# Talking-heads attention with a squared-ReLU FFN: first mixing as 64x64 array tiles, scores by way of DRAM, and one run of mixing work per tile pair

## The chip, the cores and the metric

One core of one Trainium2 chip. The metric is device time in microseconds (us) of one execution. Engine names are those of the profile: PE (matmul), PEld (its weight loads), DVE (VectorE), ACT (ScalarE), POOL (GpSimd), SP (SyncE, which here only issues DMAs). PSUM is the memory that the matmuls write; this kernel uses it as 8 banks. An eviction is the instruction on DVE or ACT that reads a result out of its bank; only then can the program give the bank to another matmul. A stream is the time in which a matmul takes in its columns, and an array mode is the size of the tiles into which the PE array is cut.

## The reference, cut to what matters

```python
# q, k, v: (8 batches, 12 heads, 448, 64); w_pre, w_post: (12, 12)
scores = scale * np.matmul(q, k.transpose(0, 1, 3, 2))
scores = np.einsum('bhij,hg->bgij', scores, w_pre)        # first mixing, over heads
attn = np.exp(scores - np.max(scores, axis=-1, keepdims=True))
attn = attn / (np.sum(attn, axis=-1, keepdims=True) + 1e-09)
attn = np.einsum('bhij,hg->bgij', attn, w_post)           # second mixing, over heads
out = np.matmul(attn, v)
# then, with x = out as (3584, 768):   h = max(x @ w_in, 0);   result = (h * h) @ w_out
```

## The kernel before

The queries of a batch are cut into 45 tiles of 10 queries. A tile has 10 queries x 12 heads = 120 rows of 448 keys. A mixing over heads is then a matmul whose contraction runs over the 120 rows, with a block-diagonal weight. There are 180 steps; each takes a pair of tiles through first mixing, and the pair of two steps earlier (LAG = 2) through second mixing. Scores for a later block, the value matmuls and the FFN are placed between.

```python
def score_pair(b, blk, p):                       # scores of two heads for a block of queries
    ...
    pss = [bank("s_ps") for _ in range(2)]       # bank() takes one of the 8 PSUM banks in turn
    for hh in range(2):
        rs = slice(64 * hh, 64 * hh + 64)
        nc.tensor.matmul(pss[hh][:, 0:S], lhsT=qTs[b][rs, p, ...], rhs=kTs[b][rs, p, :], ...)
    for hh, copy in enumerate((nc.scalar.copy, nc.vector.tensor_copy)):
        copy(out=Sb[(b, blk)][:, 2 * p + hh, :], in_=pss[hh][:, 0:S])

def gather(s):                                   # 10 query rows x 12 heads -> 120 partitions, SBUF to SBUF
    ...
    nc.sync.dma_start(out=g[0:n, :], in_=Sb[(b, blk)][x:x + n // H, :, :])

def mix(pair):                                   # first mixing: one 120x128 matmul a tile
    pss = [bank("m_ps") for _ in pair]
    for ps, s in zip(pss, pair):
        nc.tensor.matmul(ps[:, 0:S], lhsT=pre[0:n, :], rhs=Gs.pop(s)[0:n, :], start=True, stop=True)
    for ps, s in zip(pss, pair):
        nc.scalar.activation(out=e[:, :], in_=ps[:, 0:S], func=ACT.Exp, scale=SCALE, accum_out=sm[:, 0:1])
        nc.vector.reciprocal(out=rc[:, :], in_=sm[:, :])
        nc.gpsimd.tensor_scalar(out=d[:, 0:S], in0=e[:, :], scalar1=rc[:, 0:1], scalar2=-1.0 / S,
                                op0=ALU.mult, op1=ALU.add)

def unmix(pair):                                 # second mixing: rows 0-59 and 64-123 as two row tiles
    us = [bank("at_ps") for _ in range(2)]
    for x, s in enumerate(pair):
        for r in range(R):                       # R = 4
            for y in range(2):
                rows = slice(64 * y, 64 * y + HR)          # HR = 60
                nc.tensor.matmul(us[y][:, c:c + HR], lhsT=d[rows, PR * r:PR * r + P], rhs=post[rows, :], ...)
    ...
    nc.vector.tensor_copy(...)                   # two casts a pair, PSUM to bf16

for ds in range(nd + LAG):                       # the order within a step; fill() places FFN work
    ...
    mix(now2)
    fill(share)
    for w, f in now: f()                         # value matmuls, transposes
    unmix(old2)
    scores_for(ds)
    gathers_for(ds)
    fill(share)
```

The softmax here doesn't subtract the row's maximum and nothing guards it: scores larger than these inputs give would overflow.

## Time and profile before

| | before |
|---|---|
| time, median of 3 | 630.3 us (630.21 to 631.06) |
| profiled span, clock | 626.3 us, 0.964 |
| PE, DVE, ACT, POOL busy | 92%, 68%, 63%, 66% |
| first mixing, 360 matmuls | 366 ns each |
| evictions: cast of second mixing, exponential | 670 ns, 557 ns |

From the page of the profile: the span, the row of PE's busy time, the granted clock and DMA's busy share in 40 slices of the span (tenths), and the chain that ended last, by engine.

```profile
span 626.3 us, 19617 instructions
PE 576.3 (92%) x7530; PEld 323.1 (52%) x7530; DVE 423.2 (68%) x1082; ACT 396.7 (63%) x1196; POOL 410.6 (66%) x615
...
PEclk9666998999999999999999999999999999999899
DMA  9999959679547964587556964587543755322002
...
PE 61%; POOL 15%; ACT 7%; DVE 6%; DMA 5%; issue 3%; SPq 2%; ACTq 0%; DVEq 0%; POOLq 0%
```

PE is busy 92% of the span and holds 61% of the chain. In the first five slices DMA is saturated, and in the second to fourth the granted clock is lowered (0.6 of full speed).

The waits of 110 to 560 us: who waited for whom, total us, times, longest.

```profile
POOL d L325 <- DVE rc L323: 124.9, 72, 4.8
DVE rc L323 <- ACT e_sb L321: 70.3, 158, 1.6
...
PEld L346 <- issue: 39.8, 110, 0.7
...
PE s_ps L295 <- ACT e_sb L321: 2.3, 13, 0.2
...
PE m_ps L317 <- ACT hr L236: 1.5, 2, 0.8
```

PE itself (not PEld) appears only with small totals.

Two stretches in the windows view (start:end, length, then busy us of PE, PEld, DVE, ACT, POOL with counts, granted clock, DMA share, GB/s):

```profile
15.00:30.00 15.00, 6.37 (x42) 1.85 (x43) 6.10 (x15) 7.13 (x22) 3.92 (x6) 0.66 1.00 199
...
110.00:560.00 450.00, 437.98 (x5916) 240.97 (x5915) 338.74 (x851) 315.90 (x961) 313.73 (x460) 1.00 0.63 116
```

And one step on PE in the timeline (start, length, group):

```profile
312.06 0.40 PE L346 MATMUL at_ps<-post,d 60*128 60x60 bf16 x16
312.30 0.35 PE L295 MATMUL s_ps<-kT,qT 64*128 64x448 bf16 x2
312.58 0.55 PE L317 MATMUL m_ps<-G,pre 120*128 120x448 bf16 x2
313.06 1.49 PE L258 MATMUL o_ps<-w,h 128*64 128x384 bf16 x16
```

The lengths overlap (the first group lasts 0.40 us, but the next starts after 0.24), so what a group costs is the distance of starts. First mixing costs 0.48 us here: two streams of 448 columns (187 ns each) and one change of mode (about 95 ns).

### The profile page before, as it was taken

How to read it: one execution, taken by the hardware profiler on the slowest of the kernel's cores; microseconds unless marked ns; L12 is line 12 of the kernel's file. 1: busy time of each engine (PE TensorE's matmuls, PEld its weight loads, DVE VectorE, ACT ScalarE, POOL GpSimd, SP SyncE). 2: the span in 40 equal slices, each digit the busy share in tenths (PEclk: the TensorE clock that was granted, in tenths of full speed). 3: DMA queues.
4: the chain of work that ended last, by engine and by line, in shares of the span. 5: the costliest groups of instructions: out<-in, count | busy, mean ns of one | idle time of the engine just before them, and what ended most of it. 6: DMA issues, size and time to landing. Idle time of an engine off the chain costs nothing.

```text
span 626.3 us, 19617 instructions
## 1 busy us (share of the span) xinstructions
PE 576.3 (92%) x7530; PEld 323.1 (52%) x7530; DVE 423.2 (68%) x1082; ACT 396.7 (63%) x1196; POOL 410.6 (66%) x615
## 2 busy tenths in 40 slices
PE   4467898889999999999999999999999999999897
PEld 3124575645545555545545455545555555555554
DVE  3466886888777677866877677867877677654101
ACT  3456576576677657776677657776678657862320
POOL 6385969876488845895388845896387646872450
PEclk9666998999999999999999999999999999999899
DMA  9999959679547964587556964587543755322002
GB/s 141 196 197 189 183 115 159 123 110 166 136 89 117 160 135 100 101 133 113 118 103 112 157 137 98 97 136 117 122 103 74 129 122 101 75 58 76 15 12 78
DMA packets 90882, 73.64 MB, mean 118 GB/s; under 512 B 6308, under 2 KB 87716, under 8 KB 90788
## 3 DMA queue, kind: packets, MB, share of 16 engines
q1 hardware_dynamic: 51842, 49.57, 35.1%
q0 software_dynamic: 38816, 22.81, 28.2%
q8 instruction: 59, 0.97, 0.6%
q14 instruction: 35, 0.29, 0.1%
q10 hardware_dynamic: 130, 0.01, 0.0%
HBM read 45.63 MB, written 11.01 MB: 90 GB/s over the span
## 4 chain that ended last, share of the span: by engine, by line
PE 61%; POOL 15%; ACT 7%; DVE 6%; DMA 5%; issue 3%; SPq 2%; ACTq 0%; DVEq 0%; POOLq 0%
PE o_ps L258 22%; PE h_ps L228 16%; PE m_ps L317 8%; POOL d L325 6%; PE at_ps L346 5%; POOL h L237 5%; PE ot_ps L181 4%; PE s_ps L295 4%; ACT e_sb L321 3%; ACT xt L192 3%; DMA G<-S 3%; DVE at L353 2%; PE tr_ps L162 2%; DVE S L298 2%; SPq L310 2%
## 5 line engine op out<-in xcount | busy, mean ns | idle before, releaser
L325 POOL TENSOR_SCALAR d<-e_sb,rc 128x448 bf16<-128x448 f32 x360 | 226.6, 641 | 162.3 <-DVE rc L323 159.9
L321 ACT ACTIVATE e_sb<-m_ps 128x448 f32<-128x448 f32 x360 | 195.6, 557 | 77.4 <-PE m_ps L317 64.0
L353 DVE CAST at<-at_ps 112x480 bf16<-112x480 f32 x352 | 221.7, 670 | 32.7 <-PE at_ps L346 31.7
L228 PE MATMUL h_ps<-xt,w 128*128 128x448 bf16 (+2 forms) x960 | 168.5, 317 | 2.8 <-ACT e_sb L321 1.6
L258 PE MATMUL o_ps<-w,h 128*128 128x384 bf16 (+1 forms) x1024 | 162.5, 327 | 1.4 <-POOL h L237 1.3
L237 POOL TENSOR_TENSOR h<-hr 128x448 bf16<-128x448 f32 (+2 forms) x160 | 123.9, 781 | 28.5 <-ACT hr L236 25.8
L228 PEld LDWEIGHTS <-w 128*128 128x128 bf16 x960 | 82.8, 98 | 77.7 <-issue 20.9
L258 PEld LDWEIGHTS <-h 128*128 128x128 bf16 (+1 forms) x1024 | 85.3, 100 | 70.2 <-issue 15.6
L298 ACT CAST S<-s_ps 128x448 bf16<-128x448 f32 x192 | 100.0, 550 | 28.2 <-PE s_ps L295 19.9
L323 DVE RECIPROCAL rc<-sm 128x1 f32<-128x1 f32 x360 | 54.9, 159 | 91.8 <-ACT e_sb L321 89.5
L298 DVE CAST S<-s_ps 128x448 bf16<-128x448 f32 x192 | 112.8, 609 | 5.2 <-PE s_ps L295 2.9
L317 PE MATMUL m_ps<-G,pre 120*128 120x448 bf16 x360 | 104.6, 366 | 12.6 <-DMA G<-S 8.7
L236 ACT ACTIVATE hr<-h_ps 128x448 f32<-128x448 f32 (+2 forms) x136 | 68.5, 504 | 46.8 <-PE h_ps L228 31.0
L346 PEld LDWEIGHTS <-d 60*128 60x128 bf16 x2880 | 53.7, 94 | 62.6 <-issue 46.0
L295 PE MATMUL s_ps<-kT,qT 64*128 64x448 bf16 x384 | 73.6, 370 | 12.4 <-ACT S L298 7.5
L346 PE MATMUL at_ps<-post,d 60*128 60x60 bf16 x2880 | 75.0, 190 | 4.3 <-ACT xt L192 0.9
L321 ACT ACTIVATION_READ_ACCUMULATOR e_sb<-m_ps 128x1 f32 x360 | 78.1, 217 | 0.0
L192 ACT ACTIVATE xt<-ot_ps,bvec 128x160 bf16<-128x160 f32 (+3 forms) x144 | 42.6, 392 | 44.8 <-PE ot_ps L181 31.3
L317 PEld LDWEIGHTS <-pre 120*128 120x128 bf16 x360 | 29.2, 98 | 52.0 <-issue 21.3
L265 DVE COPY osb<-o_ps 128x384 f32<-128x384 f32 x48 | 26.6, 554 | 39.9 <-PE o_ps L258 39.0
L181 PE MATMUL ot_ps<-at,v 112*64 112x160 bf16 (+4 forms) x1152 | 45.9, 240 | 3.5 <-DVE at L353 3.5
L181 PEld LDWEIGHTS <-v 112*64 112x64 bf16 x1152 | 42.2, 117 | 7.6 <-issue 6.8
(36 smaller groups left out, 194.1 us busy)
## 6 DMA issues: line engine op xcount, KB each, us to landing
G<-S SPq DMA_DIRECT2D x352, 105.0 KB
kst<-in_k_dram POOLq DMA_DIRECT2D x24, 224.0 KB, 5.8
qst<-in_q_dram POOLq DMA_DIRECT2D x24, 224.0 KB, 5.9
v<-in_v_dram POOLq DMA_DIRECT2D x24, 224.0 KB, 6.2
w<-in_moe_w_in_dram POOLq DMA_DIRECT2D x8, 384.0 KB, 11.1
w<-in_moe_w_out_dram POOLq DMA_DIRECT2D x8, 384.0 KB, 7.5
out_dram<-osb SPq DMA_DIRECT2D x8, 336.0 KB
out_dram<-osb SPq DMA_DIRECT2D x8, 288.0 KB
```

Source lines behind the costliest of these rows:

```text
L181: nc.tensor.matmul(ps[64 * hh:64 * hh + 64, TW * y + c0:TW * y + 2 + n], lhsT=vs[b][0:PR, g, r, :], rhs=at[0:PR, r, g, c0:2 + n], start=(y ...
L228: nc.tensor.matmul(ps[:, 0:n], lhsT=w1[ft // 4][:, c2, ft % 4 * 128:ft % 4 * 128 + 128], rhs=xts[b][:, c2, c0:c1], start=(c2 == 0), stop=( ...
L236: nc.scalar.activation(out=hr[:, 0:n], in_=ps[:, 0:n], func=ACT.Relu)
L237: nc.gpsimd.tensor_tensor(out=h2ts[(b, ft)][:, c0:c1], in0=hr[:, 0:n], in1=hr[:, 0:n], op=ALU.mult)
L258: nc.tensor.matmul(dst, lhsT=h2ts[(b, ft)][:, mt * 128:mt * 128 + ROWS[mt]], rhs=w2[ft // 4][:, ft % 4, n2 * 384:(n2 + 1) * 384], start=(f ...
L295: nc.tensor.matmul(pss[hh][:, 0:S], lhsT=qTs[b][rs, p, BLK_START[blk]:BLK_START[blk] + P], rhs=kTs[b][rs, p, :], start=True, stop=True)
L298: copy(out=Sb[(b, blk)][:, 2 * p + hh, :], in_=pss[hh][:, 0:S])
L317: nc.tensor.matmul(ps[:, 0:S], lhsT=pre[0:n, :], rhs=Gs.pop(s)[0:n, :], start=True, stop=True)
L321: nc.scalar.activation(out=e[:, :], in_=ps[:, 0:S], func=ACT.Exp, scale=SCALE, accum_out=sm[:, 0:1])
L325: nc.gpsimd.tensor_scalar(out=d[:, 0:S], in0=e[:, :], scalar1=rc[:, 0:1], scalar2=-1.0 / S, op0=ALU.mult, op1=ALU.add)
L346: nc.tensor.matmul(us[y][:, c:c + HR], lhsT=d[rows, PR * r:PR * r + P], rhs=post[rows, :], start=True, stop=True)
L353: nc.vector.tensor_copy(out=dst[:, :, :, y, :], in_=src)
```

## The change

First mixing multiplies by a block-diagonal weight: 5 of a tile's 10 queries never meet the other 5. So half a tile (60 rows) fits one 64-row half of the array, and four such blocks (two tiles, two halves) fit the array at once. The rows must then lie at partitions 0-59 and 64-123. The gather of before was taken to be unable to give that in one access pattern, so scores are stored to DRAM and gathered from there. Second mixing is cut into 64x64 tiles as well, so that first mixing, scores and second mixing share one array mode; they are emitted as one run, and all FFN work of the step follows it.

```diff
 def score_pair(n):
+        for z, m in ((0, 64), (64, QB - 64)):
+            nc.tensor.matmul(pss[hh][z:z + m, 0:S], lhsT=qTs[b][rs, p, q0:q0 + m], rhs=kTs[b][rs, p, :], ...)
     ...
+    if p % 2:
+        nc.sync.dma_start(out=Sd[b][QB * blk:QB * blk + QB, 2 * p - 2:2 * p + 2, :], in_=Sb[0][0:QB, :, :])
 def gather(k):
+    for y in range(2):      # both tiles of the pair, one half of their queries
+        src = Sd[b][IQ * t:IQ * t + 2 * IQ, :, :].rearrange("(x y i) h j -> y (i h) x j", x=2, y=2)
+        nc.sync.dma_start(out=g[64 * y:64 * y + HR, :, :], in_=src[y])
 def mix(k):
-    for ps, s in zip(pss, pair):
-        nc.tensor.matmul(ps[:, 0:S], lhsT=pre[0:n, :], rhs=Gs.pop(s)[0:n, :], ...)
+    for y in range(2):
+        for x in range(2):
+            nc.tensor.matmul(pss[y][64 * x:64 * x + 64, 0:S], lhsT=pre[rows, :], rhs=g[rows, x, :], ...)
 def unmix(k):
-                nc.tensor.matmul(us[y][:, c:c + HR], lhsT=d[rows, PR * r:PR * r + P], rhs=post[rows, :], ...)
+                    for z in (0, 64):
+                        nc.tensor.matmul(us[x][z:z + 64, c:c + HR], lhsT=d[rows, PR * r + z:PR * r + z + 64],
+                                         rhs=post[rows, :], ...)
     ...                                          # within a step:
-            if now2:
-                mix(now2)
-            fill(share)
             for w, f in now:
                 f()
+            if now2:
+                mix(ds)
+            scores_for(ds)
             if old2:
-                unmix(old2)
+                unmix(ds - LAG)
-            scores_for(ds)
             gathers_for(ds)
             fill(share)                          # share is now the whole step's, not half
```

(Cut: constants, the building of the weights, the rule for when scores are due.)

More of the change, by code (lines that the diff above doesn't have):

```diff
@@ L23 @@
 NT = 45
-RG = H * IQ
-TPB = 12
-BLK_START = [0, 120, 240, 320]
-BLK_OFF = [0, 0, 0, 40]
-BLK_TILES = [12, 12, 12, 9]
+QB = 112
 HQ = IQ // 2
@@ L34 @@
 LAG = 2
-AHEAD = 10
+AHEAD = 6
 SCALE = 1.0 / 8.0
@@ L64 @@
     ffnp = ctx.enter_context(tc.tile_pool(name="ffnp", bufs=1))
+    dram = ctx.enter_context(tc.tile_pool(name="dram", bufs=3, space=bass.MemoryType.DRAM))
     psp = ctx.enter_context(tc.tile_pool(name="psp", bufs=8, space=bass.MemoryType.PSUM))
@@ L92, in wcol @@
         return t
-    col_pre = wcol(w_pre, "col_pre", nc.sync, [(0, IQ)])
+    col_pre = wcol(w_pre, "col_pre", nc.sync, [(0, HQ), (64, HQ)])
     col_post = wcol(w_post, "col_post", nc.scalar, [(0, HQ), (64, HQ)])
-    istripe = consts.tile([P, IQ], F32, name="istripe")
-    nc.vector.tensor_reduce(out=istripe[0:RG, :], in_=ident[0:RG, 0:RG].rearrange("p (i h) -> p i h", h=H),
-                            axis=mybir.AxisListType.X, op=ALU.add)
     hstripe = consts.tile([P, HQ], F32, name="hstripe")
@@ L104 @@
                                 axis=mybir.AxisListType.X, op=ALU.add)
-    pre = consts.tile([P, P], BF16, name="pre")
+    pre = consts.tile([P, 64], BF16, name="pre")
     nc.vector.memset(pre[:, :], 0.0)
-    for y in range(2):
-        nc.vector.tensor_tensor(
-            out=pre[0:RG, 64 * y:64 * y + HR].rearrange("p (i g) -> p i g", g=H),
-            in0=istripe[0:RG, HQ * y:HQ * y + HQ].unsqueeze(2).to_broadcast([RG, HQ, H]),
-            in1=col_pre[0:RG, :].unsqueeze(1).to_broadcast([RG, HQ, H]), op=ALU.mult)
     post = consts.tile([P, H, HQ], BF16, name="post")
@@ L115 @@
         ps = slice(p0, p0 + HR)
+        nc.vector.tensor_tensor(out=pre[ps, 0:HR].rearrange("p (i g) -> p i g", g=H),
+                                in0=hstripe[ps, :].unsqueeze(2).to_broadcast([HR, HQ, H]),
+                                in1=col_pre[ps, :].unsqueeze(1).to_broadcast([HR, HQ, H]), op=ALU.mult)
         nc.vector.tensor_tensor(out=post[ps, :, :], in0=hstripe[ps, :].unsqueeze(1).to_broadcast([HR, H, HQ]),
@@ L163, in turn_unit @@
                                         ident[0:PR, 0:PR])
+        if which == 0:
+            turned[b] = 2 * u + 2
         (eng or nc.vector.tensor_copy)(out=store[b][:, 2 * u:2 * u + 2, :],
                                        in_=ps[:, 0:2 * S].rearrange("p (y s) -> p y s", y=2))
+    turned = {}
     def turn_units(b):
@@ L284, in ffn2_units, with score_pair @@
         return u
-    Sb, Gs, dsb = {}, {}, {}
-    def score_pair(b, blk, p):
-        if (b, blk) not in Sb:
-            Sb[(b, blk)] = work.tile([P, H, S], BF16, name="S", tag="S", bufs=2)
+    Sd, Sb, Gs, dsb = {}, {}, {}, {}
+    def score_pair(n):
+        b, blk, p = n // (4 * NPAIR), n // NPAIR % 4, n % NPAIR
+        if b not in Sd:
+            Sd[b] = dram.tile([S, H, S], BF16, name="Sd", tag="Sd")
+        if p % 2 == 0:
+            Sb[0] = work.tile([P, 4, S], BF16, name="S", tag="S", bufs=3)
         pss = [bank("s_ps") for _ in range(2)]
@@ L294, in score_pair @@
             rs = slice(64 * hh, 64 * hh + 64)
-            nc.tensor.matmul(pss[hh][:, 0:S], lhsT=qTs[b][rs, p, BLK_START[blk]:BLK_START[blk] + P],
-                             rhs=kTs[b][rs, p, :], start=True, stop=True)
+            for z, m in ((0, 64), (64, QB - 64)):
+                q0 = QB * blk + z
+                nc.tensor.matmul(pss[hh][z:z + m, 0:S], lhsT=qTs[b][rs, p, q0:q0 + m], rhs=kTs[b][rs, p, :],
+                                 start=True, stop=True)
         for hh, copy in enumerate((nc.scalar.copy, nc.vector.tensor_copy)):
-            copy(out=Sb[(b, blk)][:, 2 * p + hh, :], in_=pss[hh][:, 0:S])
@@ L300, in rows_of @@
-    def rows_of(t):
-        return H * min(IQ, S - IQ * t)
-    def gather(s):
-        b, t = s
-        blk, tl = divmod(t, TPB)
-        n = rows_of(t)
-        x = BLK_OFF[blk] + IQ * tl
-        g = work.tile([P, S], BF16, name="G", tag="G", bufs=AHEAD + 2)
-        nc.sync.dma_start(out=g[0:n, :], in_=Sb[(b, blk)][x:x + n // H, :, :])
-        Gs[s] = g
-    def mix(pair):
-        pss = [bank("m_ps") for _ in pair]
-        for ps, s in zip(pss, pair):
-            n = rows_of(s[1])
-            nc.tensor.matmul(ps[:, 0:S], lhsT=pre[0:n, :], rhs=Gs.pop(s)[0:n, :], start=True, stop=True)
-        for ps, s in zip(pss, pair):
+            copy(out=Sb[0][0:QB, 2 * (p % 2) + hh, :], in_=pss[hh][0:QB, 0:S])
@@ new lines, in score_pair, with queries, needs, gather @@
+        if p % 2:
+            nc.sync.dma_start(out=Sd[b][QB * blk:QB * blk + QB, 2 * p - 2:2 * p + 2, :], in_=Sb[0][0:QB, :, :])
+    def queries(t, y):
+        return max(0, min(HQ, S - IQ * t - HQ * y))
+    def needs(s):
+        b, t = s
+        return 4 * NPAIR * b + NPAIR * ((min(IQ * t + IQ, S) - 1) // QB + 1)
+    def gather(k):
+        (b, t), (b2, t2) = pair = steps[2 * k:2 * k + 2]
+        g = work.tile([P, 2, S], BF16, name="G", tag="G", bufs=AHEAD + 1)
+        for y in range(2):
+            if b == b2 and t2 < NT - 1:
+                src = Sd[b][IQ * t:IQ * t + 2 * IQ, :, :].rearrange("(x y i) h j -> y (i h) x j", x=2, y=2)
+                nc.sync.dma_start(out=g[64 * y:64 * y + HR, :, :], in_=src[y])
+            else:
+                for x, (bx, tx) in enumerate(pair):
+                    q0, n = IQ * tx + HQ * y, queries(tx, y)
+                    nc.sync.dma_start(out=g[64 * y:64 * y + H * n, x, :],
+                                      in_=Sd[bx][q0:q0 + n, :, :].rearrange("i h j -> (i h) j"))
+        Gs[k] = g
@@ L319, in mix @@
+    def mix(k):
+        pss = [bank("m_ps") for _ in range(2)]
+        g = Gs.pop(k)
+        for y in range(2):
+            for x in range(2):
+                rows = slice(64 * y, 64 * y + H * queries(steps[2 * k + x][1], y))
+                nc.tensor.matmul(pss[y][64 * x:64 * x + 64, 0:S], lhsT=pre[rows, :], rhs=g[rows, x, :],
+                                 start=True, stop=True)
+        for y in range(2):
             e = work.tile([P, S], F32, name="e_sb", tag="E", bufs=3)
             sm = work.tile([P, 1], F32, name="sm", tag="sm", bufs=4)
-            nc.scalar.activation(out=e[:, :], in_=ps[:, 0:S], func=ACT.Exp, scale=SCALE, accum_out=sm[:, 0:1])
+            nc.scalar.activation(out=e[:, :], in_=pss[y][:, 0:S], func=ACT.Exp, scale=SCALE, accum_out=sm[:, 0:1])
@@ L322, in mix @@
             rc = work.tile([P, 1], F32, name="rc", tag="rc", bufs=4)
             nc.vector.reciprocal(out=rc[:, :], in_=sm[:, :])
-            d = dts[(NT * s[0] + s[1]) % ND]
+            d = dts[(2 * k + y) % ND]
             nc.gpsimd.tensor_scalar(out=d[:, 0:S], in0=e[:, :], scalar1=rc[:, 0:1], scalar2=-1.0 / S,
                                     op0=ALU.mult, op1=ALU.add)
-            dsb[s] = d
+            dsb[(k, y)] = d
     def place_of(s):
@@ L334, in place_of, with unmix @@
         return ats[(b, part)], 2 + IQ * (t - PARTS[b % 2][part])
-    def unmix(pair):
-        places = [place_of(s) for s in pair]
+    def unmix(k):
+        places = [place_of(s) for s in steps[2 * k:2 * k + 2]]
         us = [bank("at_ps") for _ in range(2)]
-        for x, s in enumerate(pair):
-            d = dsb.pop(s)
+        for y in range(2):
+            d = dsb.pop((k, y))
             for r in range(R):
-                for y in range(2):
-                    rows = slice(64 * y, 64 * y + HR)
-                    c = 4 * HR * x + HR * r
-                    nc.tensor.matmul(us[y][:, c:c + HR], lhsT=d[rows, PR * r:PR * r + P], rhs=post[rows, :],
-                                     start=True, stop=True)
-        (at, c), (at2, c2) = places
-        for y in range(2):
-            src = us[y][0:PR, 0:8 * HR].rearrange("p (x m i) -> p m x i", x=2, i=HQ)
-            if at is at2:
-                dst = at[0:PR, :, :, c:c + 2 * IQ].rearrange("p r g (x z i) -> p (r g) x z i", z=2, i=HQ)
-                nc.vector.tensor_copy(out=dst[:, :, :, y, :], in_=src)
-            else:
-                for x, (a, p) in enumerate(places):
-                    dst = a[0:PR, :, :, p + HQ * y:p + HQ * y + HQ].rearrange("p r g i -> p (r g) i")
-                    nc.vector.tensor_copy(out=dst, in_=src[:, :, x, :])
+                c = HR * (R * y + r)
+                for x in range(2):
+                    rows = slice(64 * x, 64 * x + HR)
+                    for z in (0, 64):
+                        nc.tensor.matmul(us[x][z:z + 64, c:c + HR], lhsT=d[rows, PR * r + z:PR * r + z + 64],
+                                         rhs=post[rows, :], start=True, stop=True)
+        for x, (at, c) in enumerate(places):
+            src = us[x][0:PR, 0:8 * HR].rearrange("p (y m i) -> p m y i", y=2, i=HQ)
+            dst = at[0:PR, :, :, c:c + IQ].rearrange("p r g (y i) -> p (r g) y i", y=2)
+            nc.vector.tensor_copy(out=dst, in_=src)
     filler = []
@@ L374, in fill @@
             owed[0] = min(owed[0], 0.0)
-    blocks = [(b, blk) for b in range(B) for blk in range(4)]
     steps = [(b, t) for b in range(B) for t in range(NT)]
@@ L383 @@
             if x > 0:
-                score_pair(0, 0, 2 * x - 2)
-                score_pair(0, 0, 2 * x - 1)
+                score_pair(2 * x - 2)
+                score_pair(2 * x - 1)
         nc.gpsimd.dma_start(out=wpost_bf[:, :], in_=w_post[0:H, 0:H])
@@ L408 @@
         nd = len(steps) // 2
-        starts = [NT * b + TPB * blk for b, blk in blocks] + [len(steps)]
         issued, gathered = [NPAIR], [0]
+        due = [(0, 0)] + [(min(k for k in range(nd) if max(needs(x) for x in steps[2 * k:2 * k + 2]) > NPAIR * n), NPAIR * n)
+                          for n in range(1, 4 * B)] + [(nd, 4 * B * NPAIR)]
         def scores_for(ds):
-            tile = 2 * ds + AHEAD + 2
-            blk = sum(tile >= x for x in starts) - 1
-            if blk + 1 >= len(blocks):
-                return
-            if blk == 3:
-                want = NPAIR * 4 + 2 * max(0, ds - FIRST_TURN[1])
-            else:
-                into, size = tile - starts[blk] - 2, starts[blk + 1] - starts[blk] - 2
-                want = NPAIR * (blk + 1) + -(-NPAIR * into // size)
-            while issued[0] < min(want, NPAIR * (blk + 2)):
-                score_pair(*blocks[issued[0] // NPAIR], issued[0] % NPAIR)
+            k = ds + AHEAD + 1
+            n = sum(k >= x for x, _ in due)
+            if n >= len(due):
+                want = due[-1][1]
+            elif n in (4, 5):
+                want = due[4][1] + 2 * max(0, ds - FIRST_TURN[1])
+            else:
+                (k0, n0), (k1, n1) = due[n - 1:n + 1]
+                want = n0 + NPAIR + -(-NPAIR * (k - k0) // (k1 - k0)) if n1 < due[-1][1] else n1
+            if n < 4:
+                want = min(want, due[4][1])
+            while issued[0] < min(want, due[-1][1]) and issued[0] % NPAIR < turned.get(issued[0] // (4 * NPAIR), 0):
+                score_pair(issued[0])
                 issued[0] += 1
         def gathers_for(ds):
-            while gathered[0] < min(2 * ds + AHEAD + 2, len(steps)):
-                b, t = steps[gathered[0]]
-                if issued[0] < NPAIR * (4 * b + t // TPB + 1):
+            while gathered[0] < min(ds + AHEAD, nd):
+                if issued[0] < max(needs(x) for x in steps[2 * gathered[0]:2 * gathered[0] + 2]):
                     break
-                gather(steps[gathered[0]])
+                gather(gathered[0])
                 gathered[0] += 1
@@ L452 @@
                 rest = 1 + min(x for x in EARLY if x >= ds) - ds
-            share = sum(w for w, _ in filler) / rest / 2 if now2 else 1e9
+            share = sum(w for w, _ in filler) / rest if now2 else 1e9
             now = timed.pop(ds, [])
-            if now2:
-                mix(now2)
-            fill(share)
             for w, f in now:
```

## The prediction

> What bounds the kernel now. The windows view of 110 to 560 us shows PE 92 to 99% busy, DVE, ACT and POOL 65 to 84%; there the list of waits has almost no PE wait above 10 us except "issue" before weight loads (40 us before second mixing, 15 and 14 before the FFN, 11 before first mixing). In the records of single matmuls this is a change of array mode: the first matmul of the other mode starts about 95 ns after the last one has streamed, some 400 times, about 39 us. The Trainium skill ("TensorEngine Tiling (Array Packing)", Key Properties) says a mode change drains the array; the trace agrees. So the middle is bound by PE streaming plus drains. The first 80 us are not: DMA share 1.0, granted clock down to 0.5, and first mixing waits for gathers.
>
> What the change does.
> 1. First mixing: two matmuls of a pair start 187 to 193 ns apart (128x128, one after the other). As four 64x64 tiles on separate rows and columns they should stream together: minus 187 ns a pair, 180 pairs, 33 us. The trace shows such overlap for two row tiles (scores, 3 ns apart) and two column tiles (transposes, 2 to 3 ns).
> 2. Scores: two matmuls become four, still one stream of 448: no change.
> 3. Second mixing: 16 weight loads and matmuls become 32. Now eight groups at 27.5 ns. The same page says column tiling loses fast weight load; the trace shows 15 ns between loads of one 128-column tile and 28 ns for a 64-column tile, two of them side by side. Eight groups at 28 ns: plus 0 to 10 ns a pair, if the sequencer keeps up with 64 instructions in 225 ns (row-tiled ones come 1.6 ns apart).
> 4. Mode changes: still two a step.
> 5. DVE, ACT, POOL: same numbers and sizes of evictions (670, 609, 550, 557, 641 ns). DVE's chain gets later, since second mixing follows at once: 3.8 us after first mixing against a step of 2.9; PSUM banks are reused about a step later, so this is close.
> 6. DMA: 38.5 MB of stores in 3584-byte packets, estimated at 175 ns from the 154 ns of 3072-byte ones: 10752 of them, 19% of 16 engines. Gathers keep size and number of packets but spread over 15 engines instead of 10, by my reading of the shapes.
> 7. SyncE queue: 360 gathers and 64 output stores at 0.87 and 0.80 us now; then about 370 gathers, 96 score stores and 64 outputs at about 0.96 with its wait: 510 us of 600. Close, but gathers run 15 us ahead.
> 8. Start: the first gather waits for a store's landing, plus 4 to 6 us, and the crowded first 80 us get 5 MB more: plus 2 to 5 us.
>
> Sum: minus 33, plus 2 for second mixing, plus 8 at the start, plus 4 from 5 and 7: about 611 us, range 596 to 630. Chances: faster 0.58, within 2% 0.27, slower 0.15.
>
> Right if: four first-mixing matmuls start within 10 ns and the next kind follows 190 ns later; second mixing spans 0.4 us; middle DMA share 0.8; few waits for gathers after 60 us.
> Wrong if: the sequencer or slow weight loads stretch second mixing to 0.6 us (plus 40 us); SyncE or DMA become the limit, shown as first mixing waiting for gathers throughout; PSUM reuse makes scores or second mixing wait for DVE; or the tiles do not run together.

## More of the kernel before

Groups of instructions on the page: busy us and mean ns of one, then idle time ahead of them and its main releaser.

```profile
L353 DVE CAST at<-at_ps 112x480 bf16<-112x480 f32 x352 | 221.7, 670 | 32.7 <-PE at_ps L346 31.7
...
L317 PE MATMUL m_ps<-G,pre 120*128 120x448 bf16 x360 | 104.6, 366 | 12.6 <-DMA G<-S 8.7
...
L346 PE MATMUL at_ps<-post,d 60*128 60x60 bf16 x2880 | 75.0, 190 | 4.3 <-ACT xt L192 0.9
```

## The result, and the profile after

| | before | after |
|---|---|---|
| median of 4 runs | 630.25 us (629.63 to 631.06) | 655.76 us (652.81 to 657.51) |
| profiled span, clock | 626.3 us, 0.964 | 651.0 us, 0.949 |

The ratio is 1.0399, 95% interval 1.0352 to 1.0446: slower by 4%, where 3% faster was predicted. A ratio here is always the mean time of one kernel's fast runs over that of the other's of the same rounds, so it is not quite the ratio of the medians quoted.

The page of the profile after:

```profile
span 651.0 us, 26878 instructions
PE 572.0 (88%) x11154; PEld 352.6 (54%) x11154; DVE 415.1 (64%) x1073; ACT 394.3 (61%) x1196; POOL 410.3 (63%) x615
...
PEclk9555898789999999999999999999999999999999
DMA  9999978959965995669755995669755576431102
...
PE 45%; POOL 16%; DVE 13%; ACT 10%; DMA 10%; issue 5%; SPq 1%; ACTq 0%; POOLq 0%; DVEq 0%
```

PE is busy about as long as before in a span that is 25 us longer. Its part of the chain fell from 61% to 45%; DVE's rose from 6% to 13%, ACT's from 7% to 10%, DMA's from 5% to 10%. Busy time of DVE, ACT and POOL did not grow: the evictions do not cost more, they are waited for more.

The same groups:

```profile
L367 DVE CAST at<-at_ps 112x480 bf16<-112x480 f32 x360 | 219.0, 642 | 3.6 <-PE at_ps L362 3.6
...
L362 PE MATMUL at_ps<-post,d 60*64 60x60 bf16 x5760 | 95.4, 196 | 14.3 <-ACT S L299 1.8
...
L331 PE MATMUL m_ps<-G,pre 60*64 60x448 bf16 x720 | 83.5, 386 | 21.6 <-DMA G<-Sd 18.3
```

DVE's cast of second mixing was preceded by 32.7 us of idle time waiting for PE; now by 3.6. Before, DVE stood ready when second mixing ended. Now the casts are late, and PE is ahead of them.

The waits of 110 to 560 us after:

```profile
POOL d L340 <- DVE rc L338: 135.1, 78, 5.5
...
DVE rc L338 <- ACT e_sb L336: 61.0, 111, 2.0
DVE S L299 <- PE s_ps L296: 40.9, 39, 2.5
...
PEld L362 <- issue: 24.6, 73, 1.4
...
PEld L331 <- DMA G<-Sd: 8.3, 24, 0.4
...
PE ot_ps L177 <- DVE at L367: 4.9, 5, 1.5
```

Waits for gathers are 8.3 us in 24 pieces of at most 0.4 us, so DMA is not the limit of the middle. The value matmuls now wait for DVE's cast, which is new. PE's other waits are split into many small lines, so the list hides their sum. I add it up below from the starts of single matmuls.

The windows of before, after:

```profile
15.00:30.00 15.00, 1.41 (x14) 0.57 (x18) 0.96 (x3) 1.50 (x5) 0.41 (x1) 0.62 1.13 256
...
110.00:560.00 450.00, 421.44 (x8626) 258.67 (x8628) 323.23 (x823) 302.37 (x932) 301.93 (x447) 0.98 0.77 187
```

From 15 to 30 us PE did 1.41 us of work instead of 6.37: the start waits longer. In the middle PE is less busy, and so is every engine but DMA. The granted clock of 0.98 comes from 110 to 170 us alone (0.82 and 0.94 in its two halves); from 170 to 560 us it is 1.00 in both kernels, so what is said of that stretch below is not the clock.

Two neighbouring steps on PE, behind value matmuls:

```profile
377.62 0.38 PE L331 MATMUL m_ps<-G,pre 60*64 60x448 bf16 x4
377.83 0.36 PE L296 MATMUL s_ps<-kT,qT 64*64 64x448 bf16 x4
378.02 0.45 PE L362 MATMUL at_ps<-post,d 60*64 60x60 bf16 x32
378.35 0.80 PE L331 MATMUL m_ps<-G,pre 60*64 60x448 bf16 x4
379.29 0.38 PE L296 MATMUL s_ps<-kT,qT 64*64 64x448 bf16 x4
379.81 0.21 PE L362 MATMUL at_ps<-post,d 60*64 60x60 bf16 x2
380.24 0.44 PE L362 MATMUL at_ps<-post,d 60*64 60x60 bf16 x30 [0.21 <-ACT S L299]
380.61 2.77 PE L254 MATMUL o_ps<-w,h 128*128 128x384 bf16 x16
```

The first step is what the change was made for: first mixing 0.21 us, scores 0.19, second mixing 0.33, all within 0.73 us. In the records its four mixing matmuls start within 10 ns (so do those of 141 of the 180 steps). No FFN work stands between these two steps, so the pair shows the loss at its worst and not in a usual step. The second step needs six PSUM banks again at once, and takes 2.26 us (380.61 less 378.35) for the same matmuls. DVE and ACT in that time:

```profile
378.27 0.62 DVE L299 CAST S<-s_ps 112x448 bf16<-112x448 f32 x1 [1.99 <-PE s_ps L296]
379.27 0.17 DVE L338 RECIPROCAL rc<-sm 128x1 f32<-128x1 f32 x1 [0.38 <-ACT e_sb L336]
379.35 0.64 DVE L367 CAST at<-at_ps 112x480 bf16<-112x480 f32 x1
379.91 0.15 DVE L338 RECIPROCAL rc<-sm 128x1 f32<-128x1 f32 x1
379.98 0.64 DVE L367 CAST at<-at_ps 112x480 bf16<-112x480 f32 x1
```

```profile
376.90 1.81 ACT L188 ACTIVATE xt<-ot_ps,bvec 128x160 bf16<-128x160 f32 x6 [2.02 <-PE ot_ps L177]
378.58 0.57 ACT L336 ACTIVATE e_sb<-m_ps 128x448 f32<-128x448 f32 x1
...
379.09 0.58 ACT L336 ACTIVATE e_sb<-m_ps 128x448 f32<-128x448 f32 x1
...
379.61 0.58 ACT L299 CAST S<-s_ps 112x448 bf16<-112x448 f32 x1
```

Read together: ACT is still at the value matmuls' results until 378.71, and in the records the second half of first mixing starts at 378.77. ACT's first exponential ends at 379.15; the scores start at 379.29. Its second ends at 379.67; second mixing gets its first bank at 379.81. Its score copy ends at 380.19, and second mixing goes on at 380.24. PE moves one bank at a time, at ACT's pace. On DVE the casts of the step before, whose data was complete by 378.47, stand behind a reciprocal that waits for the exponential: DVE is idle for 0.38 us with two finished banks in its queue, and frees them at 379.99 and 380.62.

**Where the 25 us are.** I took the start of the first exponential of each step from both traces. After runs behind before by 4.8 us at step 0, 12.4 at step 8, 16.0 at step 48, 28.1 at step 168, and 24.7 at the end. So there are two losses: 16 us up to step 48, and 12 us over the 120 steps after that, where the change should have gained 21.

For these 120 steps I split PE's time from the records of single matmuls: "stream" is columns / 2.4 in ns (448 columns take 187 to 188 ns in the trace before), divided by the number of tiles that work side by side; "mode changes" is 95 ns each; "rest" is what remains of the distance between starts.

| steps 48 to 168, us | total | stream | mode changes | rest | of it waits over 60 ns |
|---|---|---|---|---|---|
| before | 370.6 | 316.4 | 25.4 | 28.9 | 14.8 |
| after | 382.7 | 295.1 | 21.1 | 66.4 | 42.5 |

The stream fell by 21 us and the mode changes by 4; the rest grew by 37.5. Of first mixing's stream 44.8 us became 22.4, which is 187 ns a step. For each wait over 60 ns I looked up which instruction of DVE, ACT or POOL had just ended. Before: exponentials 4.9 us, value evictions 3.3, score copies 2.8, casts of second mixing 0.8. After: casts of second mixing 15.2, exponentials 11.9, ACT's score copies 6.1, value evictions 5.5. Of the 15.2, 5.6 us stand ahead of the value matmuls, which read what the cast wrote; that is a wait for data and not for a bank. The attribution is by coincidence in time, so I tested it.

Where in the emission the waits fall is as telling. After, 84 of the 120 steps stand alone between two stretches of FFN work; their runs hold only 7.5 us of the 42.5 (about 90 ns a step). The other steps follow one another without FFN work between, almost all in 15 stretches of two or three steps together with the value matmuls; these hold 26 us. The rest, 8 us, is in the FFN work. Before, the 16 stretches with value matmuls hold 9 us.

### The profile page after: what moved, and what is told of

Its sections match the earlier page's. It is cut to its first block, busy times and chain, and to the rows that moved or that the text cites. A ratio compares the mean times of both kernels' runs of the same rounds, so it can differ in the third digit from the quotient of the medians.

```text
span 651.0 us, 26878 instructions
## 1 busy us (share of the span) xinstructions
PE 572.0 (88%) x11154; PEld 352.6 (54%) x11154; DVE 415.1 (64%) x1073; ACT 394.3 (61%) x1196; POOL 410.3 (63%) x615
## 4 chain that ended last, share of the span: by engine, by line
PE 45%; POOL 16%; DVE 13%; ACT 10%; DMA 10%; issue 5%; SPq 1%; ACTq 0%; POOLq 0%; DVEq 0%
PE o_ps L254 19%; PE h_ps L224 11%; DVE at L367 7%; POOL d L340 6%; ACT e_sb L336 6%; POOL h L233 6%; DMA Sd<-S 5%; DMA G<-Sd 4%; PE ot_ps L177 4%; PE m_ps L331 4%; PE at_ps L362 3%; ACT xt L188 3%; DVE S L299 2%; PE s_ps L296 2%; PE tr_ps L154 2%
## 5 line engine op out<-in xcount | busy, mean ns | idle before, releaser
L224 PE MATMUL h_ps<-xt,w 128*128 128x448 bf16 (+2 forms) x960 | 165.2, 325 | 4.3 <-ACT S L299 1.8
L254 PE MATMUL o_ps<-w,h 128*128 128x384 bf16 (+1 forms) x1024 | 158.1, 327 | 2.8 <-POOL h L233 1.9
L299 DVE CAST S<-s_ps 112x448 bf16<-112x448 f32 x192 | 116.6, 615 | 53.2 <-PE s_ps L296 45.2
L224 PEld LDWEIGHTS <-w 128*128 128x128 bf16 x960 | 85.7, 102 | 57.4 <-issue 2.1
L362 PEld LDWEIGHTS <-d 60*64 60x64 bf16 x5760 | 87.1, 112 | 52.8 <-issue 35.3
L362 PE MATMUL at_ps<-post,d 60*64 60x60 bf16 x5760 | 95.4, 196 | 14.3 <-ACT S L299 1.8
L299 ACT CAST S<-s_ps 112x448 bf16<-112x448 f32 x192 | 101.7, 549 | 7.9 <-DMA Sd<-S 7.9
L331 PE MATMUL m_ps<-G,pre 60*64 60x448 bf16 x720 | 83.5, 386 | 21.6 <-DMA G<-Sd 18.3
L296 PE MATMUL s_ps<-kT,qT 64*48 64x448 bf16 (+1 forms) x768 | 80.4, 381 | 12.3 <-ACT S L299 4.2
L331 PEld LDWEIGHTS <-pre 60*64 60x64 bf16 x720 | 26.8, 105 | 70.8 <-issue 34.0
```

Source lines behind the costliest of these rows:

```text
L224: nc.tensor.matmul(ps[:, 0:n], lhsT=w1[ft // 4][:, c2, ft % 4 * 128:ft % 4 * 128 + 128], rhs=xts[b][:, c2, c0:c1], start=(c2 == 0), stop=( ...
L254: nc.tensor.matmul(dst, lhsT=h2ts[(b, ft)][:, mt * 128:mt * 128 + ROWS[mt]], rhs=w2[ft // 4][:, ft % 4, n2 * 384:(n2 + 1) * 384], start=(f ...
L296: nc.tensor.matmul(pss[hh][z:z + m, 0:S], lhsT=qTs[b][rs, p, q0:q0 + m], rhs=kTs[b][rs, p, :], start=True, stop=True)
L299: copy(out=Sb[0][0:QB, 2 * (p % 2) + hh, :], in_=pss[hh][0:QB, 0:S])
L331: nc.tensor.matmul(pss[y][64 * x:64 * x + 64, 0:S], lhsT=pre[rows, :], rhs=g[rows, x, :], start=True, stop=True)
L362: nc.tensor.matmul(us[x][z:z + 64, c:c + HR], lhsT=d[rows, PR * r + z:PR * r + z + 64], rhs=post[rows, :], start=True, stop=True)
```

## The experiments

The theories, with the letters that the texts use: A, the order is at fault: one run asks for six banks within 0.8 us, and evictions cannot keep pace. (From e3 on the texts part two forms of it: the bare number of banks in one run, and the queue form, in which evictions stand in DVE's order behind reciprocals that wait for the exponentials.) B, the way through DRAM. C, the 64x64 tiles themselves, by slow weight loads or too many instructions. D, too few buffers behind the exponentials. All kernels were timed against the kernel before on the same chip (629.0 to 629.4 us, median of 7), and all gave results within the comparison's tolerance, also those that leave arithmetic out. By the record's rule (2%), after, e4, e5, e7 and e9 are slower than before, e1 and e13 unclear, and all others the same; smaller differences below rest on the 95% intervals given. "Middle" is the length of steps 48 to 168 in the profiled run: 370.6 us before, 382.7 after.

### e1: the change with the order of before

```diff
-            share = sum(w for w, _ in filler) / rest if now2 else 1e9
+            share = sum(w for w, _ in filler) / rest / 2 if now2 else 1e9
+            if now2:
+                mix(ds)
+            fill(share)
             for w, f in now: ...
-            if now2:
-                mix(ds)
-            scores_for(ds)
             if old2: ...
+            scores_for(ds)
```

> The changed kernel with the emission order of before (first mixing, fill, second mixing, scores, fill) and the fill share halved again. Theory A (the one run asks for six PSUM banks within 0.8 us, so PE waits for evictions): the waits at second mixing fall from 29 us to about 8 in steps 48 to 168, two more mode changes a step (190 ns, 23 us in these steps) come back; about 635 to 645 us in all. Theory B (the way through DRAM costs the time, at the start and by load): no gain, 652 us or more. Theory C (the 64x64 tiles are slow by themselves): no gain either, second mixing stays at 0.5 us a group.

640.79 us, ratio 1.0182 (1.0149 to 1.0216); middle 373.1, with waits over 60 ns down from 42.5 to 23.3 us and about one more mode change a step (32.0 us instead of 21.1). As A expected (635 to 645 us): the one-run order costs 2.2% (1.0399 less 1.0182), some 14 us, more than the mode changes that it saves. But 1.8% remain.

### e2: only the scores' way through DRAM

The kernel before, its matmuls and its order, with scores stored to DRAM and each tile's 120 rows gathered from there (blocks of 112 queries and the rule for when scores are due are those of after):

```diff
+        if p % 2:
+            nc.sync.dma_start(out=Sd[b][QB * blk:QB * blk + QB, 2 * p - 2:2 * p + 2, :], in_=Sb[0][...])
-        nc.sync.dma_start(out=g[0:n, :], in_=Sb[(b, blk)][x:x + n // H, :, :])
+            nc.sync.dma_start(out=g[0:n, :], in_=Sd[b][IQ * t:IQ * t + n // H, :, :].rearrange("i h j -> (i h) j"))
```

> Scores through DRAM alone: matmuls, modes and order of before, gathers of 120 rows from DRAM. Theory A: the first 40 steps lose 12 to 17 us as in the changed kernel, the rest runs as before; 643 to 648 us. Theory B: also slower in steps 48 to 168, 650 us or more. If the way through DRAM costs nothing: 630 us.

637.19 us, ratio 1.0139 (1.0110 to 1.0169), less than expected. It lags by 6.1 us at step 0, 11.4 at step 6 and still 10.4 at step 168; its middle is 370.2, as before. So the way through DRAM costs 9 us, all at the start, and nothing later. From e2 to e1 it is then another 0.4%, under 3 us, and the intervals overlap: the tiles in the old order bring no gain and no clear loss. From e1 to after 2.2%. These three parts make up the 4.0%.

### e3: the run turned round

Second mixing, then scores, then first mixing, so that first mixing's banks are emptied while the FFN streams:

```diff
-            if now2:
-                mix(ds)
-            scores_for(ds)
             if old2:
                 unmix(ds - LAG) ...
+            scores_for(ds)
+            if now2:
+                mix(ds)
```

> The changed kernel with the run turned round: second mixing, scores, first mixing. The evictions of second mixing and scores then do not queue behind the reciprocals that wait for the exponentials. Theory A in the form that the VectorE queue behind the reciprocals holds the banks: PE waits for PSUM fall by half or more, 625 to 640 us. If only the number of banks in one run matters: within 1% of 655. Theories B and C: 655.

637.73 us, ratio 1.0141 (1.0124 to 1.0158); middle 371.6, rest 55.7. The same instructions, tiles and mode changes as after, in another order inside the run, are 16 us faster. That is the strongest evidence that the order costs the time, and it is within what the queue form of A expected. The other form falls: this run, too, asks for six banks at once, and for it 655 us were expected. Of the 16 us, 11 are in the middle. The text also expected the waits for PSUM to fall by half; all waits over 60 ns fall only from 42.5 to 34.9 us. Its waits of 110 to 560 us show what came instead:

```profile
DVE at L367 <- PE at_ps L362: 60.6, 70, 2.5
...
PEld L362 <- POOL d L340: 20.6, 47, 0.9
```

DVE waits for second mixing again, as in before. But second mixing now waits for POOL's scaling of the exponentials, which has less time, since second mixing stands first in the run and first mixing last. Of the waits over 60 ns (34.9 us), 8.8 end with that scaling, 6.1 with exponentials, 5.3 with value evictions, 5.2 with casts and 5.0 with POOL's squares.

### e4: second mixing as the row tiles of before

```diff
-                    for z in (0, 64):
-                        nc.tensor.matmul(us[x][z:z + 64, c:c + HR], lhsT=d[rows, PR * r + z:PR * r + z + 64], ...)
+                    nc.tensor.matmul(us[x][:, c:c + HR], lhsT=d[rows, PR * r:PR * r + P], ...)
```

> The changed kernel with second mixing as 16 row tiles of 64x128 as before; one more mode change a step. Theory C (small tiles cost): second mixing falls from 250 to 220 ns of pure stream and from 0.5 us to 0.3 a group in all, so faster than 655 by 10 us or more. Theory A: one more mode change of 95 ns a step, partly hidden in waits: 655 to 668 us.

652.47 us, ratio 1.0372 (1.0352 to 1.0392), not clearly apart from after and outside what either theory expected (A 655 to 668). Second mixing's rest falls from 29.0 to 15.1 us, but one more mode change a step takes 13 us of it back (34.3 instead of 21.1), and the middle is 383.9. C falls as the main cause. The tiles do have a price: where nothing waits, the median group of second mixing takes 43 ns more than its stream would (74 ns of rest, as in the median group of e3, instead of 31, the median before), and first mixing's 17 ns (26 instead of 9). Over 120 steps that is 7 us.

### e5 and e6: the first FFN weight loaded later, in after and in before

```diff
-            at_load(-1 if x < 4 else x - 4, load_w1, x)
+            at_load(2 * x + 1, load_w1, x)
```

> The changed kernel with the eight loads of the first FFN weight spread over tiles 1 to 15 instead of being issued before and in the first four tiles. If the loss at the start is DMA load (stores and gathers queue with the weight loads): the first exponential comes at 25 us or earlier instead of 28.7, the lead of the kernel before at step 8 falls from 12 us to 6 or less, 648 us or less in all. If it is the bare round trip through DRAM: no change at step 0, 655 us.

> Control: the same shift of the weight loads in the kernel before. If its own first gathers (6.3 us from issue to first use) also queue behind the loads: 2 to 4 us faster, about 626 us. If not, 629 us. A loss would mean that the weights come too late for the first FFN units.

e5: 650.96 us, ratio 1.0354 (1.0306 to 1.0402). e6: 634.79, ratio 1.0088 (1.0071 to 1.0106). The first exponential starts at 22.4 us in e5 and at 21.6 in e6, against 28.7 and 23.8 with the early loads. With these loads out of the way the whole change costs 0.8 us at step 0 and 0.6 at step 8, instead of 4.8 and 12.4. So the loss at step 0 is for the most part not the bare round trip but its queueing behind the weight loads, while DMA is at its limit. (At step 8 both kernels wait: e5 lags 6.7 us behind before and e6 6.1, so the 0.6 shows less.) In all, both missed: 648 us or less was expected of e5, and about 626 of e6, or 629. The loss cannot simply be moved: e6 lags 7.4 us behind before at step 48. That the weights came too late, as the text feared, its trace does not show: the first FFN matmul starts at 61.9 us (before 61.0) and waits for no weight. What e6 waits for is gathers: on the chain of work that ended last one takes 8.3 us from 41.4 us (in before 3.6 from 40.1), while the loads land, and one 6.6 us from 81.4 us, after they have landed, when the lag grows from 0.9 to 5 us. Why this second one is late stays open. (Between e5 and e6 4.4 us have come up by step 48, against 16.0; the rest is in the middle as before, 383.0 against 370.4.)

### e7 and e8: lighter evictions

No accumulator read on ACT, the reciprocal taken of a constant, casts of half the columns; in after (e7) and in before (e8).

```diff
-            nc.scalar.activation(out=e[:, :], in_=..., func=ACT.Exp, scale=SCALE, accum_out=sm[:, 0:1])
+            nc.scalar.activation(out=e[:, :], in_=..., func=ACT.Exp, scale=SCALE)
-            nc.vector.reciprocal(out=rc[:, :], in_=sm[:, :])
+            nc.vector.reciprocal(out=rc[:, :], in_=one[:, :])
-            nc.vector.tensor_copy(out=dst, in_=src)
+            nc.vector.tensor_copy(out=dst[:, 0:2 * H], in_=src[:, 0:2 * H])
```

> Wrong result on purpose: the changed kernel with lighter evictions. The reciprocal takes a constant instead of the sum of the exponentials (no accumulator read on ScalarE, no wait on it in VectorE's queue) and the casts after second mixing copy half the columns. PE work is untouched. Theory A (evictions hold the PSUM banks, PE waits): PE waits over 100 ns in steps 48 to 168 fall from 51 us to under 15, 615 to 628 us in all. Theory C (64x64 matmuls are slow by themselves): 650 us or more.

> Wrong result on purpose: the same lighter evictions in the kernel before. Theory A: its PE waits are only 18 us in these steps, so it gains 5 to 15 us, 615 to 625 us, and the changed kernel with the same evictions is level with it or ahead after the start. Theory C: the distance between the two stays 25 us.

Both missed. e7: 668.08 us, ratio 1.0621 (1.0586 to 1.0656), with 18% less busy time on DVE (338.6 us instead of 415.1) and yet the slowest kernel of all. e8: 632.40, ratio 1.0058 (1.0034 to 1.0083), where a gain was expected; its middle is 377.4, longer by 6.8 than that of before. The groups of e7 show why:

```profile
L338 DVE RECIPROCAL rc<-one 128x1 f32<-128x1 f32 x360 | 57.0, 161 | 182.9 <-POOL d L340 181.9
```

Freed of its input, the reciprocal now runs ahead and then waits for POOL to free one of its four output buffers, for 181.9 us in all, at the head of DVE's queue. The casts stand behind it: waits over 60 ns that end with a cast rise from 15.2 to 23.3 us, and the middle from 382.7 to 398.1. The experiment did not measure what it was meant to, but it shows that what stands at the head of a queue can matter more than how much work is in it.

### e9 and e10: more buffers

```diff
-        hr = ffnp.tile([P, S], F32, name="hr", tag="hr", bufs=2)
+        hr = ffnp.tile([P, S], F32, name="hr", tag="hr", bufs=3)
-            e = work.tile([P, S], F32, name="e_sb", tag="E", bufs=3)
-            sm = work.tile([P, 1], F32, name="sm", tag="sm", bufs=4)
+            e = work.tile([P, S], F32, name="e_sb", tag="E", bufs=6)
+            sm = work.tile([P, 1], F32, name="sm", tag="sm", bufs=8)
-            rc = work.tile([P, 1], F32, name="rc", tag="rc", bufs=4)
+            rc = work.tile([P, 1], F32, name="rc", tag="rc", bufs=8)
```

> The changed kernel with deeper buffers behind the first mixing: exponentials 3 to 6, sums and reciprocals 4 to 8, ReLU results 2 to 3. Theory D, formed from the last runs (the second exponential waits for GpSimd to free one of three buffers, so ScalarE holds its PSUM bank and PE waits): ScalarE waits for GpSimd (14 us in 110 to 560 us) vanish, PE waits over 100 ns in steps 48 to 168 fall from 51 us to 35 or less, 635 to 645 us. If only the order of evictions matters (theory A): 652 to 656 us.

> Control: the same deeper buffers in the kernel with scores through DRAM and the matmuls of before (637 us; the kernel before itself has no room for them). Its ScalarE hardly waits for GpSimd, so theory D expects 633 to 637 us.

e9 (on after): 650.60 us, ratio 1.0333 (1.0285 to 1.0381), middle 384.8: outside both ranges. e10 (on e2; the kernel before has no room for these buffers): 636.60, ratio 1.0126 (1.0087 to 1.0165), as expected. D falls: ACT's waits for POOL's scaling shrink from 14.1 us to 4.4 in 110 to 560 us, but PE's waits over 60 ns stay (44.5 us).

### e11 and e12: the best parts together, and a control

e3 with the buffers of e9 and the first FFN weight's loads one a tile; e12 has these loads alone, in before.

```diff
-            at_load(-1 if x < 4 else x - 4, load_w1, x)
+            at_load(x + 1, load_w1, x)
```

> Candidate: run turned round (637.7 us), deeper buffers, first FFN weight loaded one piece a tile from tile 1. Theory D with the start relieved: 615 to 628 us, faster than the kernel before. If nothing adds up: 636 us.

> Control for the candidate: the kernel before with the same weight loads, one piece a tile from tile 1. First exponential at 21.6 us as in the later shift (before 23.8) without the later loss of 6 us: 626 to 629 us.

Both missed. e11: 632.37 us (629.79 to 633.36, 6 runs), ratio 1.0057 (1.0028 to 1.0085): the fastest with 64x64 first mixing, 23 us faster than after, still not faster than before. Its middle is 371.6 as in e3. e12: 637.43, ratio 1.0131 (1.0105 to 1.0158): of the three places tried for the loads (before, e6, e12), that of before is the best for it.

### e13 and e14: no reciprocals

This is what e7 was to be: DVE never waits for an exponential, since POOL scales by a constant.

```diff
-            rc = work.tile([P, 1], F32, name="rc", tag="rc", bufs=4)
-            nc.vector.reciprocal(out=rc[:, :], in_=sm[:, :])
-            nc.gpsimd.tensor_scalar(out=d[:, 0:S], in0=e[:, :], scalar1=rc[:, 0:1], scalar2=-1.0 / S,
+            nc.gpsimd.tensor_scalar(out=d[:, 0:S], in0=e[:, :], scalar1=1.0 / S, scalar2=-1.0 / S,
```

> Wrong result on purpose: the changed kernel without the reciprocals; GpSimd scales by the constant 1/448. VectorE's queue then holds nothing that waits for ScalarE or GpSimd. Theory A in its queue form (casts of second mixing wait in VectorE's order behind reciprocals that wait for the exponentials, so PSUM banks come free late): PE waits that end with such a cast fall from 15 us to under 4 in steps 48 to 168, 634 to 644 us in all. If the bursts alone matter: 648 us or more.

> Control, wrong result on purpose: the kernel before without the reciprocals. Its PE waits hardly ever for casts (0.8 us), so 624 to 629 us.

e13: 640.62 us, ratio 1.0182 (1.0142 to 1.0222). e14: 619.87, ratio 0.9856 (0.9828 to 0.9883), more than expected. In after, waits that end with a cast fall from 15.2 to 4.5 us and the middle from 382.7 to 374.9 (by 7.8). The time is as expected (634 to 644 us); so the attribution to the casts holds, and DVE's queue behind the reciprocals is a real part. But before gains 4.4 us in its middle from the same edit, so only 3.4 us are special to the change, and after stays about 21 us behind its control. The control says something the prediction denied: with PE's stream and mode changes untouched, the middle of before became 4.4 us shorter. It was not bound by PE alone.

### e15 and e16: one more step between the mixings

e11 with LAG 3 (e15), and e3 with LAG 3 (e16), so that second mixing need not wait for the scaling.

```diff
-LAG = 2
+LAG = 3
```

> Candidate: the run turned round, deeper buffers, weight loads one a tile (632.4 us), and second mixing three steps behind the first instead of two. In the turned run PE waits 8.8 us for GpSimd's d in steps 48 to 168; with one step more they vanish: 620 to 628 us. If other waits take their place: 632 us.

> The turned run with three steps of lag, buffers and weight loads as in the changed kernel (637.7 us with two steps). Parted from e15 by the start alone: 625 to 633 us, 4 to 6 us behind e15.

e15: 637.06 us (633.91 to 642.42), ratio 1.0137 (1.0081 to 1.0194), a miss. e16: 633.26 (632.34 to 640.34), ratio 1.0102 (1.0036 to 1.0169), and ahead of e15, against the expectation; their runs overlap. Waits for the scaling are gone in e15 (8.8 us in e3, 0.2 here), but those that end with POOL's squares are now 9.8, with exponentials 6.5, with value evictions 5.3. e16's middle is 369.5, the shortest with 64x64 tiles, and 1 us below that of before.

### Not tried

More PSUM banks cannot be given: all 8 are in the rotation already. Nor can the waits on them be left out without a race. Not tried, though within reach: FFN work between the steps that follow one another beside the value matmuls, where most of the waits of after stand; and the gather within SBUF in two halves.

## Why the prediction was wrong, point by point

**Item 1, first mixing: right, mechanism and size.** Four matmuls start within 10 ns (in 141 of 180 steps; in the others they waited apart) and the next kind 203 ns after the last of them; the stream falls by 187 ns a step.

**Items 2, 4 and 6: right.** Scores keep their stream (23.7 us before, 23.9 after, in the 120 steps). Mode changes fell a little, from 406 to 324 in the run, of about 95 ns. This gap agrees with the Trainium skill ("TensorEngine Tiling (Array Packing)", Key Properties), which says that changing the mode drains the engine. The 3584-byte packets took 177 ns where 175 was estimated, and DMA's middle share is 0.77 where 0.8 was.

**Item 3, second mixing: undersized.** Plus 0 to 10 ns a pair was said; it was 43 ns where nothing waits. It spans 0.45 us, and the 0.6 us named as the danger did not come. e4 bounds it: not the cause.

**Item 7, SyncE: wrong, to the good.** Issue was to take 0.96 us and 510 us in all. Without its waits it took 0.51 us a gather and 0.37 a score store; with the outputs about 260 us in all, less than the 366 of before, counted the same way.

**Item 8, the start: undersized.** Plus 4 to 6 and 2 to 5 us were summed to 8. After lags 12.4 us at step 8 and 16.0 at step 48. The way through DRAM alone accounts for about 9 us of the final time (e2), which fits the 8; at step 0 its mechanism is crowding with the weight loads (e5, e6). The further 5 us up to step 48 go with the change's matmuls and their order (e1 lags 14.8 there, e3 12.4). The granted clock was lower from 110 to 140 us in after, 0.82, than in e2, 0.97; whether that is cause or consequence was not tested.

**The step that failed: item 5 and the "plus 4 from 5 and 7".** The text named the danger itself ("this is close", and under "Wrong if": "PSUM reuse makes scores or second mixing wait for DVE"), and gave it at most 4 us with SyncE. PE's waits over 60 ns grew by 28 us in 120 of 180 steps, and rest as a whole by 37.5. Two things were overlooked. First, the order: e1 and e3 show that the same matmuls cost 14 to 16 us less when the six banks of a step are not asked for as after asks for them. The change gathers PE's short work, each piece of which fills two banks in 0.2 to 0.33 us, while emptying one bank takes ACT or DVE 0.55 to 0.64 us. It is just the long FFN stretches, 2.6 us for one or two banks, that give evictions time to catch up. Where they still stand between the steps, the waits of the run are small; where steps follow one another beside the value matmuls, 26 of the 42.5 us are lost. The number of banks alone does not decide: e3 asks for as many in one run, with second mixing first and the exponentials left to be emptied under the FFN. Second, which engine waits was misjudged: item 5 looked at DVE alone. After e3 had relieved DVE, POOL's scaling, its squares, exponentials and value evictions took its place.

**Under it lies the premise**, "the middle is bound by PE streaming plus drains". If it held, 21 us less stream and 4 us fewer mode changes, less 7 us for the price of the small tiles, would have come through at least in e3, where the order is mended. There the middle is 371.6 us against 370.6. A PE that is busy 97% of the middle (437.98 of 450 us) was read as the only limit. e14 shows that the other engines were a limit beside it. The Trainium skill has the general point ("TensorEngine Tiling (Array Packing)", PSUM Bottleneck): "Tiling speeds up TensorE but not PSUM evacuation". The exponential took 557 ns before and 553 after, the cast 670 and 642; DVE, ACT and POOL were busy for 67 to 75% of 110 to 560 us in both kernels, in bursts, and none of the nine kernels with 64x64 first mixing that kept the arithmetic whole got the middle below 369.5 us.

What stays open: how the waits of the mended order (e3, 34.9 us) share out among POOL, ACT and DVE. Each relief moved them to another releaser, and attribution by coincidence cannot say what a relief of all would give. No version tried beats the kernel before; the nearest, e11, is 0.6% behind.

## What to carry to other kernels

Before a saving on PE is counted, ask who empties its PSUM banks, how many banks the new order asks for within one eviction time, and what stands at the head of each evicting queue; a PE that is 97% busy can have a second limit right beneath it. When short pieces of PE work are put together to save mode changes, see where no long work is left between them that gave evictions time, and try the order inside the run, since here that alone moved the time by 16 us. A round trip through DRAM that is free in the steady state can still cost at the start, when it queues with the first weight loads.

## What the Trainium skill lacked or had wrong

- "TensorEngine Tiling (Array Packing)", Key Properties, says that a mode change drains the array but gives no cost: here about 95 ns from the end of the last stream to the first matmul of the other mode, on 324 to 406 changes a run.
- The same page, Restrictions, says that column tiling disables Fast Weight Load but not what that costs: second mixing with 64x64 tiles spent a median of 74 ns over its stream on its eight groups of four, against 31 ns with row tiles (where nothing waits; the number of matmuls and loads doubled too, so the loads need not be all of it). The gain of Fast Weight Load stands in "TensorE: Matmul & The Clock Gate", but not for such tiles. The PSUM Bottleneck section of the tiling page is right, but it speaks only of a copy that is too slow; here each engine had time to spare and the order and the heads of the queues made the waits (e3: 16 us by order alone; e7: slower with less work).
- "DMA: Bandwidth & Descriptors", Why a DMA increments its semaphore by 16 and not by 1 (under "How many engines (k)"), gives the number of engines of a transfer (by its rule 10 for the gathers of before, whose slowest dimension is 10 queries, and 15 for those of after with 60 rows). The trace does not show a packet's engine, but the 4-byte packets on SyncE's queue, 4618 before and 8186 after, are as many as the rule gives when each engine of a transfer writes one. No page gives the time that an issue on SyncE takes by the shape of the transfer (the one count of cycles for a copy stands in the part on another chip, as that of earlier generations): a gather took 0.87 us before and 0.51 after, and the output stores, whose shapes did not change, 0.80 and 0.49. Which property of the gathers makes the difference was not told apart; it is not the two halves, since those of e2, of 120 rows from DRAM, took 0.44.
